# Chunked attention and a top-2 mixture of experts: the rest list summed by routing group in the last attention slot, turned tiles amid the first products, and nine result rows' puts behind the overflow branch

## The chip, the cores and the metric

The kernel runs on one core of a Trainium2 chip. The metric is the device time of one execution in microseconds (us). Engines are named as the profile does: PE (matmul; PEld its weight loads), DVE, ACT, POOL and SP; a q behind a name is that engine's sequencer. POOL issues all gathers and scatters (indirect DMAs), SP the transposing DMAs and the direct stores.

## The reference

First an attention over chunks of 32 queries, each of which sees 8 memory keys and the keys from 16 before its chunk to 8 behind it; then a mixture of experts over the 3072 tokens that come out.

```
q, k, v: 4 batches x 8 heads x 768 x 64;  mem_k, mem_v: 8 keys each
for each chunk c: a = softmax(q_c . [mem_k, k_ctx] / 8);  out_c = a . [mem_v, v_ctx]
x = out as (3072, 512)
noisy = x @ w_gate + log1p(exp(x @ w_noise)) * noise          # 8 experts
top2 of noisy per token, their weights by softmax over the two
for e in 8 experts, for the tokens that chose e:
    out[token] += weight * (relu(x[token] @ w1[e]) @ w2[e])   # 512 -> 1024 -> 512
```

## The kernel before, in words

**Phase 1** runs 12 attention tiles in slots. In each slot a string of short codes (`ORDERS`) says in which order the pieces of work are written, and each engine runs its instructions in that order. Tokens are routed in three groups of tiles: tiles 0 to 6, 7 to 9, and 10 to 11 (the last group, whose tiles carry names such as `d_last`, `vals_last`). The last slot's string holds the routing of groups 1 and 2.

**Sorting.** The tokens are listed by the pair of experts that they chose (28 pairs). The first 96 tokens of a pair make one ordinary tile; `main_src` holds the token numbers of each tile's rows, as sums of one-hot matrices times facts (`p_list`). Tokens beyond the 96 of their pair are the rest. They are listed in the same way: `rest_onehots` (L1204 to L1207) makes one-hots of 64 rest positions for all 24 subtiles of 128 tokens at once, `rest_list` (L1214) multiplies them with the facts in 24 matmuls, the sum is copied to `tsb` and stored to `tdr` in DRAM, and 16 small gathers (`rest_facts`) bring each expert's rest entries to `fr`. `rest_decode` makes of them the row numbers from which to read (`rs`), those to which to write (`rd`, in pieces `dA` and `dB`) and the weights; `rest_rows` gathers the rows. If any count is too large for its place, `flag` is above zero, and a branch behind everything else runs `overflow()`, which repairs the result.

**Phase 2** goes through the experts. `gathers` brings token tiles from `xd` in DRAM into `xt` (POOL, L938, one indirect DMA per tile), a tile is turned, that is transposed, either by an SP transposing DMA or by PE with a copy (`turn_pe`, L1148 and L1149), `mm1` (L992) makes the hidden rows (relu at L978 on DVE, L980 on ACT), `mm2_tiles` (L1054) the results. A pair's tile is made once by each of its two experts; the second one adds (L1063) and its rows are put to the output (`put`, L943, POOL). Rest rows are added to what the output holds: `clear_prev` clears `pA` and `pB` (ACT, L1124), `get_prev` reads the rows (POOL, L969), `ins_` adds them (`yB` L1108, `yr` L1117) and `put_rest` (L960) writes them back. Four tiles of opposite pairs (names `yq`, `QP`) are finished by `finish_q` (L1085, L1086). `later` is the list of finished rows whose puts `flush` issues.

The head of phase 2 is written out by hand (L1385 on): seven gathers, the counts and tables of the rest (`rest_counts`, `rest_tables`), the rest one-hots, tile 0 turned and multiplied, tiles 1 and 2 turned, the rest list, a product over tiles 1 and 2 (192 columns), tile `QP` turned, the 32-column products, the three tiles of `i0` turned, and then the product over these three (288 columns). For the last expert (e = 7) the rest rows are put first and then the three results of `in_of(7)`, before the branch; behind the branch, which stands in `tc.If(nov > 0)` and is taken or not by all engines, stand the three results of `out_of(7)` and the last `yq`.

A wait in this kernel is a count that an engine's instruction waits for; an instruction that waits holds all that is behind it on its engine. PE, ACT, DVE, SP and POOL all run in the written order here.

Of the kernel before, what the change touches and what calls it, by code (L numbers as in the profile page):

```python
# [22 lines left out]
def kernel(  # L23
# [73 lines left out]
    NV = 6  # L97
# [85 lines left out]
    radr = const.tile([128, 2, E], F32, name="radr")  # L183
    rslot28 = const.tile([128, 2], F32, name="rslot28")
# [80 lines left out]
    class Route:  # L265
# [397 lines left out]
    def decode(L, n, name, src=None, pool=const):  # L663
# [42 lines left out]
    ]  # L706

    with tc.manual_schedule(engines={ET.PE, ET.Activation, ET.DVE, ET.SP}):
# [32 lines left out]
        def slot(i):  # L741
# [133 lines left out]
            for k in ORDERS[i + 1].split():  # L875
# [4 lines left out]
                elif k == "p2":  # L880
                    p2 = new_list(NV - 2)
                elif k == "a":
# [14 lines left out]
            if i == NT - 1:  # L897
                add_list(p1, 0, 1)
                add_list(p2, 1, NV - 1)

# [83 lines left out]
    def mm1(e, cols, x, sinks, engs=(0, 1)):  # L984
        fk = 1 if cols > 256 else 2 if cols > 128 else 4
        for f0 in range(0, FB, fk):
            p = psH.tile([128, 512], F32, name="p_h")
            for f in range(f0, f0 + fk):
                o = p[:, (f - f0) * cols:(f - f0 + 1) * cols]
                for kp in range(KP):  # L990
# [3 lines left out]
                                     start=(kp == 0), stop=(kp == KP - 1))  # L994
            for c0, c1, to in sinks:
# [54 lines left out]
    def mm2_tiles(e, ps, h, unit):  # L1050
        for k, g in enumerate(ps):
# [9 lines left out]
            else:  # L1061
# [3 lines left out]
                later.append((y[0:MT], dst[0:MT, g:g + 1]))  # L1065

    def flush():
        for y, ix in later:
            put(y, ix)
        later.clear()  # L1070

    def outs(e):
        unit = yqp.tile([128, Dm], F32, name="yq") if e < 4 else yrp.tile([128, Dm], F32, name="yr")
        mm2_tiles(e, out_of(e), hO, unit)
        if e < 4:
            yq[e] = unit
        else:
            yr_of[e] = unit

    def finish_q(e):  # L1080
        if e >= 4:
# [3 lines left out]
            nc.vector.tensor_scalar(out=y, in0=y, scalar1=wl[0:MT, 0, q:q + 1], scalar2=None, op0=Alu.mult)  # L1085
            last[0] = nc.vector.scalar_tensor_tensor(out=y, in0=unit[0:MT], scalar=wl[0:MT, 1, q:q + 1], in1=y, op0=Alu.mult, op1=Alu.add)  # L1086
            later.append((y, dst[0:MT, q:q + 1]))
# [6 lines left out]
    def ins_(e):  # L1094
# [18 lines left out]
        put_rest(rest_tile(), dB, outB, 2 * N)  # L1113
# [4 lines left out]
        put_rest(unit[0:MT], dA, out, N)  # L1118
# [25 lines left out]
    def turn_pe(g, to, n=MT):  # L1144
# [4 lines left out]
        nc.scalar.copy(to, p)  # L1149
# [8 lines left out]
    tsb = late.tile([RU, NP, 8], F32, name="tsb")  # L1158
    oh_at = scol[0] + 4096
    oh_t = wflat[:, oh_at:oh_at + NG * RU].rearrange("p (g t) -> p g t", g=NG)  # L1160
# [10 lines left out]
    def rest_tables(p, part):  # L1171
# [28 lines left out]
        nc.vector.tensor_copy(nxt, flag)  # L1200

    def rest_onehots():
        t1 = late.tile([128, NG], F32, name="t1")
        nc.vector.tensor_scalar(out=t1, in0=rank, scalar1=float(MT), scalar2=None, op0=Alu.is_ge)  # L1204
        k2 = late.tile([128, NG], F32, name="k2")
# [317 lines left out]
```

## Time and profile before

| what | us |
|---|---|
| median of 3 runs (lowest to highest) | 346.47 (346.16 to 347.88) |
| the profiled execution's own time | 349.4 |
| its span, first to last instruction | 347.8 |
| PE busy (80% of the span) | 278.9 |
| POOL busy (58%) | 203.4 |
| DVE busy (53%) | 183.6 |
| ACT busy (45%) | 155.0 |

The profiled execution took 2.9 us longer than the median, and 1.6 us of its own time lie outside its span. Phase 1 lasts to about 130 us, the head of phase 2 to about 150; from there PE works nearly without a pause until 329, and the span ends at 347.8 with nothing but POOL's puts behind it. The mean granted clock of TensorE is 0.918. Shares of busy time are averages over these stages, so a change is to be read from the stage that it touches. In the profile's rows the first number is the start in us, the second the duration in us; brackets hold how long the engine was idle before and what released it.

### The profile page before, as it was taken

The page shows a single profiled execution, that of the slowest core. Times are in us where ns is not written, and L with a number is a line of the kernel's source. Part 1 is how long each engine was busy: PE and PEld are TensorE (multiplying, and loading weights), DVE is VectorE, ACT ScalarE, POOL GpSimd, SP SyncE. Part 2 cuts the span into 40 slices and gives each one's busy share as a digit, 9 for nine tenths or more (in the row PEclk, how much of TensorE's full clock was granted, in tenths as well). Part 3 has the DMA queues.
Part 4 walks back from the last instruction along what each step waited for, and adds up shares of the span by engine and source line. Part 5 has one row for each costly group of instructions (what it writes and reads, how often), then busy time and mean ns, then how long its engine had stood idle before and what let it go on. Part 6 is the DMA issues. An engine that isn't in the chain of part 4 may idle for free.

```text
span 347.8 us, 9190 instructions
## 1 busy us (share of the span) xinstructions
PE 278.9 (80%) x3746; PEld 207.2 (60%) x3762; DVE 183.6 (53%) x406; ACT 155.0 (45%) x320; POOL 203.4 (58%) x291
## 2 busy tenths in 40 slices
PE   0678788766777746797999999999999999999800
PEld 0557677655667636656668766676676666866300
DVE  4675568676499677236363533644345354353500
ACT  4657638553565312534445363553443534534200
POOL 4669679982046247745777776571745735626531
PEclk9978899998899556999999999999999999999955
DMA  7999969999516512421686996999999699504221
GB/s 127 211 211 179 224 111 210 192 168 161 106 28 107 140 31 59 109 59 47 114 119 139 160 127 158 185 217 166 186 150 198 159 170 157 152 25 118 79 77 45
DMA packets 43277, 46.78 MB, mean 135 GB/s; under 512 B 20241, under 2 KB 33621, under 8 KB 43228
## 3 DMA queue, kind: packets, MB, share of 16 engines
q0 software_dynamic: 22800, 38.26, 58.8%
q1 hardware_dynamic: 19884, 7.83, 11.6%
q8 instruction: 31, 0.51, 0.6%
q14 instruction: 18, 0.15, 0.1%
q10 hardware_dynamic: 544, 0.03, 0.1%
HBM read 59.11 MB, written 11.33 MB: 203 GB/s over the span
## 4 chain that ended last, share of the span: by engine, by line
PE 44%; issue 6%; DMA 5%; DVE 4%; POOL 2%; ACT 2%; POOLq 1%; DVEq 0%; ACTq 0%
PE p_h L992 23%; PE p_y L1054 17%; DMA pB<-out_dram,ri 4%; POOL out_dram L943 2%; PE p_y L1102 2%; ACT w_all L1149 1%; DMA xt<-xd,main_src 1%; ACT w_all L980 1%; PE p_xt L1214 1%; DVE yq L1048 0%; POOLq L1518 0%; PE p_x L623 0%; POOL out_dram L960 0%; PE p_xt L1148 0%; PE p_list L372 0%
## 5 line engine op out<-in xcount | busy, mean ns | idle before, releaser
L992 PE MATMUL p_h<-w_all 128*128 128x288 bf16 (+3 forms) x1120 | 96.1, 248 | 4.0 <-ACT w_all L1149 2.8
L992 PEld LDWEIGHTS <-w_all 128*128 128x128 bf16 x1120 | 83.1, 99 | 17.7 <-issue 5.9
L1054 PE MATMUL p_y<-w_all 128*128 128x512 bf16 x368 | 83.6, 379 | 1.7 <-ACT yr L1048 0.5
L980 ACT ACTIVATE w_all<-p_h 128x288 bf16<-128x288 f32 (+3 forms) x137 | 46.8, 375 | 51.8 <-PE p_h L992 50.3
L1054 PEld LDWEIGHTS <-w_all 128*128 128x128 bf16 x384 | 37.0, 98 | 43.3 <-issue 1.8
L412 POOL COPY w_all<-w_all 128x512 bf16<-128x512 bf16 (+1 forms) x59 | 42.0, 781 | 13.0 <-PE p_t L432 8.4
L978 DVE TENSOR_SCALAR w_all<-p_h 128x288 bf16<-128x288 f32 (+1 forms) x65 | 30.7, 476 | 35.5 <-PE p_h L992 34.0
L938 POOL DMA_INDIRECT xt<-xd,main_src x28 | 27.0, 963 | 10.1 <-issue 7.3
L1063 DVE SCALAR_TENSOR_TENSOR y<-p_y,main_w,y 96x512 f32<-96x512 f32 x24 | 17.9, 747 | 24.8 <-PE p_y L1054 24.8
L943 POOL DMA_INDIRECT out_dram<-y,main_dst x24 | 22.5, 936 | 12.6 <-issue 6.1
L1048 ACT COPY yr<-p_y 32x512 f32<-32x512 f32 x24 | 13.9, 579 | 35.6 <-DVE y L1063 34.5
L960 POOL DMA_INDIRECT out_dram<-yB,rd x8 | 9.8, 1226 | 28.6 <-DVE yB L1108 28.0
L1059 ACT ACTIVATE y<-p_y,main_w 96x512 f32<-96x512 f32 x24 | 16.4, 682 | 21.2 <-PE p_y L1054 20.1
L432 PE MATMUL p_t<-identf,w_all 128*128 128x128 f32 x120 | 20.6, 314 | 1.3 <-ACT pT L587 0.8
L938 POOL DMA_INDIRECT xt<-xd,rs x16 | 14.8, 924 | 11.3 <-DVE rw L1246 6.3
L1048 DVE COPY yr<-p_y 32x512 f32<-32x512 f32 x12 | 8.3, 694 | 22.3 <-ACT y L1059 21.3
L614 DVE TENSOR_TENSOR w_all<-ps_o,rs 128x512 bf16<-128x512 f32 x24 | 15.7, 683 | 6.5 <-PE ps_o L601 5.6
L1223 POOL DMA_INDIRECT fr<-tdr,adr x16 | 16.1, 1007 | 4.9 <-issue 4.9
L461 PE MATMUL p_v<-identf,w_all 128*128 128x128 f32 x96 | 15.9, 305 | 2.7 <-ACT w_all L436 1.8
L432 PEld LDWEIGHTS p_t<-identf,w_all 128*128 128x128 f32 x120 | 15.9, 163 | 2.7 <-POOL w_all L412 1.4
L587 ACT COPY pT<-p_p 128x1024 bf16<-128x1024 bf16 x11 | 11.1, 1012 | 12.7 <-PE p_p L581 12.4
L501 DVE TENSOR_REDUCE mx<-ps_s 128x16 f32<-128x1024 f32 x12 | 14.7, 1223 | 2.8 <-PE ps_s L488 2.5
(231 smaller groups left out, 405.2 us busy)
## 6 DMA issues: line engine op xcount, KB each, us to landing
w_all<-in_moe_w_dram POOLq DMA_DIRECT2D x16, 1024.0 KB
w_all<-in_k_dram POOLq DMA_DIRECT2D x4, 768.0 KB
w_all<-in_q_dram POOLq DMA_DIRECT2D x4, 768.0 KB
w_all<-in_v_dram POOLq DMA_DIRECT2D x4, 768.0 KB
xd<-w_all SPq DMA_DIRECT2D x24, 128.0 KB
w_all<-mvn SPq DMA_DIRECT2D x24, 32.0 KB
w_all<-xt SPq DMA_TRANSPOSE x39
xt<-xd,main_src POOLq DMA_INDIRECT x28
```

Source lines behind the costliest of these rows:

```text
L412: i = eng.tensor_copy(to, x)
L432: nc.tensor.transpose(out=p_t[:, s, :], in_=m.bitcast(F32)[:, s * 128:(s + 1) * 128], identity=identf)
L938: pin(nc.gpsimd.indirect_dma_start(out=t[0:n].bitcast(I32), out_offset=None, in_=src_, in_offset=bass.IndirectOffsetOnAxis(ap=ix, axis=0)))
L943: i = nc.gpsimd.indirect_dma_start(out=out if rows is None else rows, out_offset=bass.IndirectOffsetOnAxis(ap=ix, axis=0), in_=y, in_offse ...
L978: nc.vector.tensor_scalar(out=out_, in0=in_, scalar1=0.0, scalar2=None, op0=Alu.max)
L980: nc.scalar.activation(out=out_, in_=in_, func=Act.Relu)
L992: nc.tensor.matmul(out=o if len(xk.shape) == 2 else o.rearrange("p (j t) -> p j t", j=xk.shape[1]), lhsT=w_all[:, e % WR, kp * F + f * 128 ...
L1048: (nc.scalar.copy if eng else nc.vector.tensor_copy)(to, p[MT:128, :])
L1054: nc.tensor.matmul(out=p, lhsT=h[:, f, k, :], rhs=w2(e, f), start=(f == 0), stop=(f == FB - 1))
L1059: nc.scalar.activation(out=y[0:MT], in_=p[0:MT], func=Act.Copy, scale=wt)
L1063: nc.vector.scalar_tensor_tensor(out=y[0:MT], in0=p[0:MT], scalar=wt, in1=y[0:MT], op0=Alu.mult, op1=Alu.add)
L1223: i = nc.gpsimd.indirect_dma_start(out=fr[0:n, b, e], out_offset=None, in_=tdr, in_offset=bass.IndirectOffsetOnAxis(ap=adr[0:n, b, e:e + 1 ...
```

## The change

- The rest list is made by routing group. `rest_onehots(r)` and `rest_list(r, p)` take one group; codes `I0`, `I1`, `I2` (one-hots of group 0, 1, 2) and `T0`, `T1`, `T2` (their matmuls) stand in the last slot's string, the sum stays in a PSUM tile of phase 1 and is copied to `tsb` at the slot's end. The store of `tsb` is SP's first work of phase 2.
- In the head, tile 0 is turned first. Tiles 1, 2, `QP` and `i0` are turned amid the matmuls of the product before them (`amid`), some of the copies go to DVE.
- `away` is −128 where `flag` is zero, and far out of the output's rows where it is not, so that rest rows are not put when the branch will be taken.
- For e = 7 the puts of the three `in_of(7)` results, of `yB` and of `yr` move behind the branch, where there are nine instead of four. For e = 6 the three results are put ahead of the rest rows. `scale_q` (L1085 of before) stands ahead of `outs(e)`.
- The first part of the rest's decode stands amid `outs(0)`, the rest rows' gathers follow it ahead of one tile of `in_of(1)`, and the rest rows of expert 0 are turned amid `mm1_rest(1)`.

```diff
-        "P N p X C1 C1 V i x v G X2 ... H2 O2 q2 a B2 F2",
+        "P N p X C1 C1 V i I0 x v G X2 ... H2 O2 I1 q2 T0 T1 a B2 F2 I2 T2",
...
+    def rest_onehots(r):
+        t1 = keep.tile([128, r.n], F32, name=f"t1{r.k}")
+        nc.vector.tensor_scalar(out=t1, in0=r.rr, scalar1=float(MT), scalar2=None, op0=Alu.is_ge)
+        k2 = keep.tile([128, r.n], F32, name=f"k2{r.k}")
+        nc.vector.scalar_tensor_tensor(out=k2, in0=r.rr, scalar=1.0 - MT, in1=t1, op0=Alu.add, op1=Alu.mult)
+        nc.vector.tensor_tensor(out=oh_t[:, r.g0:r.g0 + r.n], in0=bc(k2, RU),
+                                in1=io_1[:, 0:RU].unsqueeze(1).to_broadcast([128, r.n, RU]), op=Alu.is_equal)
+    def rest_list(r, p):
+        for s in range(r.n):
+            g = r.g0 + s
+            nc.tensor.matmul(out=p, lhsT=oh_t[:, g], rhs=r.vals[:, s], start=(g == 0), stop=(g == NG - 1))
...
             if i == NT - 1:
                 add_list(p1, 0, 1)
                 add_list(p2, 1, NV - 1)
+                nc.vector.tensor_copy(tsb[:, :, 0:NV], p_rest.rearrange("p v c -> p c v"))
...
-    def mm1(e, cols, x, sinks, engs=(0, 1)):
+    def mm1(e, cols, x, sinks, engs=(0, 1), amid={}):
...
+                if f in amid:
+                    amid[f]()
...
-        put_rest(rest_tile(), dB, outB, 2 * N)
+        if e == E - 2:
+            flush()
+        yB = rest_tile()
+        later_rest = [partial(put_rest, yB, dB, outB, 2 * N), partial(put_rest, unit[0:MT], dA, out, N)]
+        if e < E - 1:
+            later_rest.pop(0)()
...
-        put_rest(unit[0:MT], dA, out, N)
+        if e < E - 1:
+            later_rest.pop(0)()
+        later.extend(later_rest)
...
+        nc.vector.tensor_scalar(out=away, in0=flag, scalar1=float(BIG), scalar2=-128.0, op0=Alu.mult, op1=Alu.add)
...
-        nc.vector.scalar_tensor_tensor(out=t, in0=t, scalar=-128.0, in1=u, op0=Alu.add, op1=Alu.max)
+        nc.vector.scalar_tensor_tensor(out=t, in0=t, scalar=away, in1=u, op0=Alu.add, op1=Alu.max)
...
+        rest_store()
+        turn_pe(0, xs[:, 0])
         p_cnt = rest_counts()
         rest_tables(p_cnt, 0)
-        rest_onehots()
-        turn_pe(0, xs[:, 0])
-        mm1_main(0, [0], hO, engs=(0,))
-        turn_pe(1, xs[:, 1])
-        turn_pe(2, xs[:, 2])
-        p_t = rest_list()
-        mm1(0, 2 * MT, ..., engs=(0,))
-        turn_pe(QP, x3[0][:, :, 0:MT])
-        mm1_rest(0, r=False, engs=(0,))
-        nc.vector.memset(tsb, 0.0)
+        mm1_main(0, [0], hO, engs=(0,), amid={3: lambda: turn_pe(1, xs[:, 1], eng=0), 5: lambda: turn_pe(2, xs[:, 2])})
         rest_tables(p_cnt, 1)
-        rest_store(p_t)
...
+        mm1(0, 2 * MT, ..., engs=(0,),
+            amid={1: lambda: turn_pe(QP, x3[0][:, :, 0:MT]), 4: lambda: turn_pe(i0[0], xs[:, i0[0]], eng=0),
+                  6: lambda: turn_pe(i0[1], xs[:, i0[1]], eng=0)})
         next(dec)
+        mm1_rest(0, r=False, engs=(0,), amid={3: lambda: turn_pe(i0[2], xs[:, i0[2]], eng=0)})
         dst, wl = next(dec)
-        for g in i0:
-            turn_pe(g, xs[:, g])
...
-        i1 = gathers(in_of(1))
-        outs(0)
+        i1 = gathers(in_of(1), 2)
         dx = rest_decode(0, 2)
-        next(dx)
-        next(dx)
+        outs(0, amid={1: lambda: next(dx)})
         rest_rows(0)
+        i1 += gathers(in_of(1))
         rest_rows(1)
+        next(dx)
...
             if n == E:
                 ins_(e)
-                flush()
+            scale_q(e)
             outs(e)
```

**DVE at the end of the last slot.** Here `d_last`, `facts` and `vals_last` are the last group's facts, `listed` the sums of the lists. Before:

```order
L336 TENSOR_TENSOR d_last<-d_last,facts 128x4
L334 CAST facts<-d_last 128x4
L337 TENSOR_TENSOR facts<-ii_last 128x4
L366 TENSOR_TENSOR vals_last<-ohp,facts 128x4x112
L384 TENSOR_TENSOR listed<-listed,p_list 96x28
L384 TENSOR_TENSOR listed<-listed,p_list 96x112
L1174 TENSOR_SCALAR cnt_2956<-p_xt 128x64
```

After:

```order
L341 TENSOR_TENSOR d_last<-d_last,facts 128x4
L339 CAST facts<-d_last 128x4
L342 TENSOR_TENSOR facts<-ii_last 128x4
L371 TENSOR_TENSOR vals_last<-ohp,facts 128x4x112
L387 TENSOR_SCALAR t_2946<-rank 128x4
L389 SCALAR_TENSOR_TENSOR k_2948<-rank,t_2946 128x4
L390 TENSOR_TENSOR w_all<-k_2948,io_128 128x256
L402 TENSOR_TENSOR listed<-listed,p_list 96x28
L402 TENSOR_TENSOR listed<-listed,p_list 96x112
L925 COPY tsb<-ps_o 64x28x6
L1214 TENSOR_SCALAR cnt_2999<-p_xt 128x64
```

The one-hots of the last group's rest (L387 to L390) and the copy to `tsb` stand ahead of the counts. In the built program the first gather of phase 2 (POOL) waited for DVE's count behind `main_src`; now it waits for the count behind L390, since its tile `xt` lies where `k_2948` lay.

**ACT at the head of phase 2.** The L1149 rows of before and the L454 rows of after with `p_xt` are copies of turned tiles. Before:

```order
L1149 COPY w_all<-p_xt 128x384
L980 ACTIVATE w_all<-p_h 128x4x96 x2
L1149 COPY w_all<-p_xt 128x384 x2
L980 ACTIVATE w_all<-p_h 128x2x2x96 x4
L1149 COPY w_all<-p_xt 128x4x96
L980 ACTIVATE w_all<-p_h 128x12x32 x2
L679 ACTIVATE main_w<-main_w 128x56
L1149 COPY w_all<-p_xt 128x384 x3
L980 ACTIVATE w_all<-p_h 128x3x96 x4
```

After:

```order
L454 COPY w_all<-p_xt 128x384
L1006 ACTIVATE w_all<-p_h 128x4x96
L454 COPY w_all<-p_xt 128x384
L1006 ACTIVATE w_all<-p_h 128x4x96
L454 COPY w_all<-p_xt 128x4x96
L1006 ACTIVATE w_all<-p_h 128x2x2x96 x4
L697 ACTIVATE main_w<-main_w 128x56
L1006 ACTIVATE w_all<-p_h 128x12x32 x2
L1006 ACTIVATE w_all<-p_h 128x3x96 x4
```

Tile 2 is copied between the two relus of tile 0's product, `QP` ahead of the first relu of the 192 columns, and the four copies of tile 1 and `i0` are gone to DVE.

**POOL at the tail.** `pA` and `pB` are the reads of the rows that the rest is added to, `nxt` is the flag as a number. Before:

```order
L969 DMA pA<-out_dram,ri_4379 96x512
L969 DMA pB<-out_dram,ri_4379 128x256
L960 DMA out_dram<-yB,rd_4377 6144x256
L960 DMA out_dram<-yr,rd_4377 3072x512
L943 DMA out_dram<-y,main_dst 3072x512 x3
L1488 TENSOR_LOAD nxt
L1490 COMPARE_AND_BRANCH
...
L943 DMA out_dram<-y,main_dst 3072x512 x3
L943 DMA out_dram<-yq,main_dst 3072x512
```

After:

```order
L995 DMA pA<-out_dram,ri_4391 96x512
L995 DMA pB<-out_dram,ri_4391 128x256
L1506 TENSOR_LOAD nxt
L1508 COMPARE_AND_BRANCH
...
L969 DMA out_dram<-y,main_dst 3072x512 x3
L986 DMA out_dram<-yB,rd_4389 6144x256
L986 DMA out_dram<-yr,rd_4389 3072x512
L969 DMA out_dram<-y,main_dst 3072x512 x3
L969 DMA out_dram<-yq,main_dst 3072x512
```

Five puts moved from ahead of the branch to behind it, and the branch now follows the read of `pB`.

More of the change, by code (lines that the diff above doesn't have):

```diff
@@ L1 @@
 import math
+from functools import partial
 from contextlib import ExitStack
@@ L1157 @@
     nxt = late.tile([128, 1], I32, name="nxt")
-    tsb = late.tile([RU, NP, 8], F32, name="tsb")
-    oh_at = scol[0] + 4096
-    oh_t = wflat[:, oh_at:oh_at + NG * RU].rearrange("p (g t) -> p g t", g=NG)
+    away = late.tile([128, 1], F32, name="away")
     def rest_counts():
@@ L1435 @@
         load_next()
-        for b, n, c in ((0, MT, MT), (1, RU, 2 * MT)):
-            turn_pe(("r", 0, b), x3[0][:, :, c:c + n], n)
         turn_rest(1)
```

62 lines of the change are left out of this document (33 added, 29 removed), and 2 rows, old and new, of the table ORDERS.

## The prediction

> **What bounds the kernel now.** I read the table of stretches first (us, then busy time of PE, PEld, DVE, ACT, POOL, the granted clock, DMA share and GB/s), then the chain of waits through the head of phase 2, then the rows around the branch.
>
> ```profile
> 118.50:123.50 5.00, 2.72 (x29) 2.35 (x30) 4.25 (x14) 1.39 (x5) 4.04 (x10) 0.50 0.19 43
> ...
> 130.40:137.30 6.90, 4.56 (x62) 4.18 (x62) 5.42 (x22) 1.20 (x3) 5.60 (x5) 0.50 0.20 58
> 137.30:147.10 9.80, 7.28 (x110) 6.79 (x108) 3.66 (x20) 5.69 (x14) 7.40 (x8) 1.00 0.44 107
> ...
> 182.50:300.00 117.50, 116.75 (x1020) 79.62 (x1028) 53.15 (x107) 53.07 (x133) 71.52 (x74) 1.00 0.93 168
> ...
> 330.00:347.80 17.80, 0.00 (x0) 0.00 (x0) 1.12 (x2) 0.58 (x1) 4.16 (x5) 0.55 0.22 65
> ```
>
> From 182.5 to 300 PE is the bound (116.75 of 117.5 us), and the change touches nothing there: what is won or lost ahead of 182.5 goes through to the end unshortened. It can act in three places. In the last slot DVE is the bound (4.25 of 5.00 us). In the head PE works 11.8 of 16.7 us and waits for tiles and copies. From 330 on PE is idle, and 17.8 us belong to POOL. The head, by the chain of waits (its small steps of issue between these lines are left out):
>
> ```profile
> 130.44 2.71 DMA xt<-xd,main_src
> 133.20 0.52 PE p_xt L1148 x4
> 133.79 0.49 ACT w_all L1149
> 134.31 2.73 PE p_h L992 x32
> 137.46 0.48 ACT w_all L1149
> 137.98 1.90 PE p_xt L1214 x24
> 139.88 2.76 PE p_h L992 x32
> 143.15 0.38 ACT w_all L1149
> 143.57 1.53 PE p_h L992 x32
> 146.18 0.34 PE p_xt L1148 x4
> 147.08 4.08 PE p_h L992 x32
> ```
>
> Tile 0 is gathered, turned, copied, multiplied; then PE stands while ACT copies the next tile, and so on. From the landing of tile 0 (130.44 + 2.71 = 133.15) to the first product of `in_of(0)` at 147.08 it is 13.93 us. The tail, POOL's rows and the last result of DVE by the timeline, then the sequencer's instructions of the branch (L1490) and of the end (L1518), with count, shortest, median and longest in ns and first and last start:
>
> ```profile
> 319.75 1.03 POOL L969 DMA_INDIRECT pB<-out_dram,ri  x1 [0.30 <-issue]
> 324.21 1.27 POOL L960 DMA_INDIRECT out_dram<-yB,rd  x1 [3.42 <-DVE yB L1108]
> 325.78 0.95 POOL L960 DMA_INDIRECT out_dram<-yr,rd  x1 [0.30 <-issue]
> 329.49 1.00 POOL L943 DMA_INDIRECT out_dram<-y,main_dst  x1 [0.30 <-issue]
> 335.41 0.92 POOL L943 DMA_INDIRECT out_dram<-y,main_dst  x1 [4.92 <-DVEq L1490]
> 339.08 0.92 POOL L943 DMA_INDIRECT out_dram<-yq,main_dst  x1 [0.30 <-issue]
> 330.63 0.75 DVE L1086 SCALAR_TENSOR_TENSOR yq<-yr,main_w,yq 96x512 f32<-96x512 f32 x1 [0.25 <-ACT yr L1048]
> ```
>
> ```profile
> L1490 POOLq EVENT_SEMAPHORE  x6: 17/30/43, 329.9 to 332.6; - x6
> L1490 POOLq COMPARE_BRANCH  x1: 58/58/58, 327.2 to 327.2; - x1
> L1490 POOLq INC_SWDGE_SEM  x1: 1795/1795/1795, 332.7 to 332.7; - x1
> L1518 POOLq DRAIN  x3: 46/109/9904, 337.0 to 347.5; - x3
> ```
>
> The branch costs POOL 4.92 us in which it does nothing. It compares at 327.2, its next instruction stands at 329.9 (2.6 us later), then six semaphore waits go to 332.6, which is 3.2 us after the last put ahead of the branch began (329.49), then INC_SWDGE_SEM takes 1.80 us to 334.5, and 0.9 us later the first put behind the branch starts. I read the waits as those for the landing of everything that POOL issued before. The last result is ready at 330.63 + 0.75 = 331.38, so the end is set by POOL's branch and its four puts. The long DRAIN begins at 337.0 (337.0 + 9.9 is 346.9, and a later start would not fit into the span), 6.9 us past the last put's end at 340.0.
>
> **The change, part by part.**
>
> *Tail: the branch is taken earlier.* Ahead of the branch now stands the read of `pB` (319.75) as the last transfer. The nearest rows for its landing are 2.71 us (the first gather) and 3.2 us (the last put): 322.5 to 323.0. POOL's compare can follow that read's issue at about 320, plus 2.6 us to the next instruction gives 322.7, much the same. So INC starts at about 322.8, ends at 324.6, and the first put starts at 325.5. Nine puts follow. Each `y` starts 1.22 us after the one before (0.92 + 0.30), `yB` takes 1.57 (1.27 + 0.30) and `yr` 1.25: three `y` 3.66, `yB` and `yr` 2.82, three `y` 3.66, together 10.1 us to the start of the last, 335.6 instead of 339.08. That is −3.4. The results are there in time: `yB` before 324.21 (its put began then), `yq` at 331.4. Bounds: −3.9, if the pieces lie closer, to −2.5, if the wait behind the branch costs a further us.
>
> *Smaller pieces of the tail.* `scale_q` leaves DVE's end; nothing follows, since `yq` waits for its turn on POOL. For e = 6 the three `y` are put ahead of the rest rows, and `pA` waits for `yr` to land; POOL has 3.42 us idle ahead of `yB` before, and the read of `pA` waits for the same `clear_prev` on ACT either way. Zero; if that cover were gone, the read of `pB`, and so the branch, would come later by about one put, 1.22 us.
>
> *Last slot: one-hots added on DVE.* These rows price them:
>
> ```profile
> 127.91 0.56 DVE L359 TENSOR_TENSOR oh_l_last<-rank,io_l 128x384 bf16<-128x384 f32 x1
> 129.37 0.18 DVE L883 TENSOR_TENSOR main_src<-p_list,listed 96x28 int32<-96x28 f32 x1 [0.91 <-PE p_list L372]
> 130.56 0.16 DVE L337 TENSOR_TENSOR facts<-ii_last 128x4 bf16<-128x4 f32 x1
> 130.76 0.63 DVE L366 TENSOR_TENSOR vals_last<-ohp,facts 128x448 bf16<-128x448 bf16 x1
> 133.04 0.21 DVE L1204 TENSOR_SCALAR t<-rank 128x24 f32<-128x24 f32 x1
> 133.29 0.18 DVE L1206 SCALAR_TENSOR_TENSOR k<-rank,t 128x24 f32<-128x24 f32 x1
> 133.50 1.76 DVE L1207 TENSOR_TENSOR w_all<-k,io 128x1536 bf16<-128x1536 f32 x1
> ...
> 130.44 1.05 POOL L938 DMA_INDIRECT xt<-xd,main_src  x1 [1.89 <-DVE d_last L336]
> ```
>
> 384 columns take 0.56 and 1536 take 1.76, about 1.04 ns per column. `I0` (896 columns) is 0.21 + 0.18 + 1.09 = 1.48, written into the stretch where DVE has 0.75 of 5.00 us idle: +1.4 (bounds +0.7 and +1.5). `I1` (384 columns) is 0.95 and falls into the 0.91 us idle ahead of `main_src`: +0.1. `I2` (256 columns, 0.43 + 0.39 = 0.82) stands behind `vals_last`, and by the order of the built program the first gather waits for it, since its tile lies on the memory of the one-hots' input. Before, the gather started at 130.44, 0.89 us after `main_src` (129.55); the count that it waits for is that of `main_src`, though the row names a later DVE instruction. Now DVE comes through `facts` and `vals_last` to 131.4 and through `I2` to about 132.1 (the pieces overlap by 0.1), and with the same 0.89 the gather starts at 133.0 instead of 130.44: +2.6 (bounds +1.7 without the 0.89, +2.7). Together the first gather moves by +4.1. The matmuls of `T0` to `T2` (24 of 79 ns, from 1.90 us) lie beside DVE's work.
>
> *Head: turned tiles amid the products.* From the landing of tile 0 in the new order: turning 0.52, copy 0.49, gaps 0.09, then 2.73 for tile 0's product with two turnings amid it (0.52 each at the half clock, 0.34 at the full: 0.9 together), then 2.76 for the 192 columns with three turnings (1.0), then 1.53 + 0.34 for the 32 columns with one, and about 0.3 of gaps: 10.6 instead of 13.93. Gone are the 1.90 of the rest list and three copies on which PE stood (0.48, 0.38 and 0.49 with the gaps around them). −3.3; bounds −2.3 (one copy or one landing still waited for in each product) and −3.9. The gathers of `i0` follow each other like the puts, about 1.22 us apart, and fall due about when they are turned. The rest's tables stand behind tile 1's copy on DVE; the `i0` copies stand behind those tables, about 20 small instructions of 0.2, and PE's next tile hides them as long as the 192 columns last. Together slot and head: +0.8 (bounds −1.0 and +2.0).
>
> *Clock of the head.* In the table PE's granted clock is 0.50 up to 137.3 and 1.00 from there, 4.1 us after the turning of tile 0 began at 133.20. I take the same 4.1 us at half clock from the new start. The Trainium skill (TensorE: Matmul & The Clock Gate, Part 1) says that the gate opens only after a busy window of about 3.4 us, and that the windows run freely, so that the place of the change depends on where work begins in a window. By that rule the cold stretch lies between 3.4 and 6.8 us, the row's 4.1 fits it, and the sum would be up to 1.2 us longer in an execution that starts unluckily; only the change of clock at 137.3, in one execution, is shown here.
>
> *Rest decode and rest rows.*
>
> ```profile
> 158.95 0.21 ACT L1249 ACTIVATE rx<-rx 128x8 f32<-128x8 f32 x1 [1.82 <-DVE rx L1248]
> ...
> 159.51 0.77 PE L992 MATMUL p_h<-w_all 128*128 128x288 bf16 x5 [1.14 <-ACT w_all L980]
> ...
> 164.27 0.92 PE L992 MATMUL p_h<-w_all 128*128 128x160 bf16 x11 [0.89 <-ACT w_all L1149]
> ```
>
> PE waits 1.14 us at 159.51 for a relu that ACT reaches only after an exponential of the decode (L1249, itself 1.82 us late), and 0.89 at 164.27 for copies of the rest rows. With the decode's first part amid `outs(0)` and the turnings amid the products a part of both goes: −0.35 each, −0.7 in all (bounds 0, if POOL's gathers or the transposes behind them are late next, and −1.5). The extra `away` is one DVE instruction of about 0.2 on a flag that nobody waits for before the tail: hidden. The store of `tsb`, first on SP's queue now, waits for DVE's copy; SP has no transposes due until later in the head.
>
> *Sum.* Tail −3.4, slot and head +0.8, rest −0.7: −3.3 us. The profiled execution took 349.4, its span 347.8; the changed one comes to a span of 344.5. The profiled one lies 2.9 above the median of 346.47, so I take the difference to the median: 346.47 − 3.3 = 343.2.
>
> **Rivals.**
>
> 1. *The first put behind the branch is released by DVE's branch, not by POOL's own.* Its row names DVEq L1490, and that instruction and POOL's INC end together at 334.5, so times alone can't tell them apart. Then nothing is won by an earlier compare: DVE's branch can't come before its last result, the first put stays at 335.4, and five more puts (3 × 1.22 + 1.57 + 1.25 = 6.5) follow: 349.7 with the other terms, slower. Against it: in the built program that put waits for DVE's count of the `y`, which stands below that of `yq`, and for a DMA count that INC raises. The same sign would come from a DRAIN that grows with the number of puts behind the branch: its 6.9 us by four puts are 1.7 each, five more are +8.7, and above 0.7 each the gain is lost. Nothing varies that number in the trace.
> 2. *The later gather isn't bought back.* If PE still waits for landings or copies in the head, its gain is the bound −2.3 (1.0 worse); if the decode's waits only move to POOL's gathers, 0.7 is lost as well; both give 344.9, no change that can be told, and with a half clock that lasts a window's part longer still more. For it speaks that the head's gathers come one by one from POOL, 4.1 us later than before; against it, that PE's waits there are for copies in the quoted rows of the chain and for a landing only in the first.
> 3. *The tail gains less.* If something else holds the branch (the landing of `pA`, or a branch target that takes longer than 2.6 us), by 1.5 us: 344.7.
> 4. *The front gains as well.* If `I0` falls into DVE's idle time (+0.7) and decode and head reach their good bounds, 343.2 − 0.7 − 0.6 − 0.8 = 341.1.
>
> **How the numbers follow.** 0.5% is 1.73 us, about what a measurement of this kernel can tell from no change: below 344.74 is faster, above 348.2 slower. My forecast, 342.0 to 344.5, has 0.56; rival 4 has 0.10, all faster; rival 3 has 0.12, two thirds of it faster; rival 2 has 0.14, a quarter of it faster; rival 1 has 0.08, all slower. Faster 0.56 + 0.10 + 0.08 + 0.03 = 0.77, slower 0.08, no change 0.15. The range reaches from rival 4 with a little more on its side, 340.5, to the upper part of rival 2, 345.8; what it leaves out is rival 1 and tails of 2 and 4, under 0.2.
>
> **What would show it.** In the profile after: the first put behind the branch near 325.5 plus the shift of the front, nine puts to about 335.6, and the end 6.9 us past the last; the first gather near 134.5; the stretch from its landing to the 288-column product near 10.6 us; no L1214 of before between products. The prediction is wrong if the first put behind the branch waits for the end of DVE's work, if the DRAIN is longer than 9 us past the last put, or if PE shows waits for copies by DVE in the head.

## The result

The changed kernel took 343.62 us (median of 20 runs, 341.86 to 347.81), the kernel before beside it 348.67 (20 runs, 346.16 to 351.90). The ratio is 0.9871, 95% interval 0.9843 to 0.9898: 1.0 to 1.6% faster. On the median of 346.47 that the forecast started from, the ratio gives 342.0; forecast were 343.2, with a range of 340.5 to 345.8. The profiled execution's span went from 347.8 to 343.7 us.

The tail of the changed kernel, POOL's timeline from the reads of `pA` and `pB` on, then the sequencer's instructions at the branch (now L1508) and at the end (L1536):

```profile
317.31 1.00 POOL L995 DMA_INDIRECT pA<-out_dram,ri  x1 [3.93 <-ACT pA L1166]
318.61 1.04 POOL L995 DMA_INDIRECT pB<-out_dram,ri  x1 [0.30 <-DVE y L1091]
324.55 0.96 POOL L969 DMA_INDIRECT out_dram<-y,main_dst  x1 [4.91 <-DVE yq L1114]
...
329.58 1.45 POOL L986 DMA_INDIRECT out_dram<-yr,rd  x1 [0.30 <-issue]
...
335.01 0.92 POOL L969 DMA_INDIRECT out_dram<-yq,main_dst  x1 [0.31 <-issue]
```

```profile
L1508 POOLq EVENT_SEMAPHORE  x6: 17/30/43, 321.4 to 321.9; - x6
...
L1508 POOLq COMPARE_BRANCH  x1: 58/58/58, 318.3 to 318.3; - x1
...
L1508 POOLq INC_SWDGE_SEM  x1: 1695/1695/1695, 321.9 to 321.9; - x1
...
L1508 DVEq EVENT_SEMAPHORE  x1: 21/21/21, 333.3 to 333.3; - x1
...
L1536 POOLq DRAIN  x3: 46/109/12603, 330.3 to 343.4; - x3
```

POOL compares at 318.3, its INC runs from 321.9 to 323.6, and the first of nine puts starts at 324.55. The read of `pB` began at 318.61, and the six semaphore instructions at the branch take 0.5 us (321.4 to 321.9), where before they took 2.7 us (329.9 to 332.6), with puts issued just ahead of them: in the changed kernel next to nothing is left to wait for there. DVE's instruction of the branch, which the row of before named as the releaser, stands at 333.3, 8.7 us after the first put. The last put ends at 335.93 and the span 7.8 us later, as before (339.99 and 347.8).

The head, by the chain of waits (small steps of issue left out):

```profile
133.41 2.75 DMA xt<-xd,main_src
136.20 0.50 PE p_xt L1190 x4
...
137.31 1.44 PE p_h L1018 x16
138.75 0.32 PE p_xt L1190 x4
139.07 0.64 PE p_h L1018 x8
139.71 0.32 PE p_xt L1190 x4
140.03 2.00 PE p_h L1018 x16
...
145.89 4.70 PE p_h L1018 x48
```

The last row joins two things: the second half of the 32-column products (16 matmuls) and the product over `in_of(0)` (32 matmuls of 288 columns). In PE's timeline the latter begins at 146.50:

```profile
146.50 0.42 PE L1018 MATMUL p_h<-w_all 128*128 128x288 bf16 x2
```

The copies by ACT that stood between the products of before are gone from the chain; in these rows a turning costs PE its own 0.32 (0.17 at the full clock) and nothing more.

Phase 1 takes a different time in each execution: the reciprocal with which DVE begins the part of the last slot that is compared here stood between 114.6 and 119.9 us in the fourteen profiles, the kernel before at 118.46. Whole spans of single executions are therefore compared by stretches between six landmarks of the timeline: that reciprocal (R), the start of the first gather of phase 2 (G), the first result product (Y), the end of the last matmul (Z), the end of the last put (T), the end of the span (E).

| us | R to G | G to Y | Y to Z | Z to T | T to E | sum |
|---|---|---|---|---|---|---|
| before | 11.98 | 20.77 | 177.99 | 10.80 | 7.80 | 229.34 |
| changed | 15.71 | 17.02 | 177.62 | 7.88 | 7.77 | 226.00 |
| difference | +3.73 | −3.75 | −0.37 | −2.92 | −0.03 | −3.34 |

In these two executions the front takes and gives the same, and what is won is the tail. In the second, third and fourth sets of runs every kernel, the one before too (medians 432.65, 432.25 and 433.84 us), took some 80 us longer than in the first; of these only stretches that are free of it are read.

### The profile page after: what moved, and what is told of

The parts are those of the page before. It is cut to its first block, busy times and chain, and to the rows that moved or that the text cites. A ratio compares the mean times of both kernels' runs of the same rounds, so it can differ in the third digit from the quotient of the medians.

```text
span 343.7 us, 9215 instructions
## 1 busy us (share of the span) xinstructions
PE 285.3 (83%) x3762; PEld 212.9 (62%) x3762; DVE 185.8 (54%) x417; ACT 153.6 (45%) x316; POOL 203.2 (59%) x291
## 4 chain that ended last, share of the span: by engine, by line
PE 47%; DMA 11%; DVE 9%; issue 6%; POOL 3%; ACT 2%; POOLq 1%; DVEq 0%; ACTq 0%
PE p_h L1018 21%; PE p_y L1082 15%; DMA w_all<-in_moe_w_dram 3%; DMA fr<-tdr,adr 2%; DMA out_dram<-yr,rd 2%; DMA w_all<-mvn 2%; PE p_t L450 2%; PE p_y L1137 1%; DMA pB<-out_dram,ri 1%; POOL out_dram L969 1%; PE ps_o L396 1%; DVE w_all L632 1%; POOL out_dram L986 1%; PE ps_s L506 1%; PE p_x L641 1%
## 5 line engine op out<-in xcount | busy, mean ns | idle before, releaser
L1018 PE MATMUL p_h<-w_all 128*128 128x288 bf16 (+3 forms) x1120 | 98.0, 249 | 1.5 <-ACT w_all L1006 0.9
L1082 PE MATMUL p_y<-w_all 128*128 128x512 bf16 x384 | 85.9, 379 | 1.0 <-DVE yq L1076 0.6
L964 POOL DMA_INDIRECT xt<-xd,main_src x28 | 26.2, 936 | 12.8 <-issue 7.6
L479 PE MATMUL p_v<-identf,w_all 128*128 128x128 f32 x96 | 16.6, 315 | 2.5 <-ACT w_all L454 1.8
L454 ACT COPY w_all<-p_v 128x512 f32<-128x512 f32 x21 | 11.9, 588 | 8.1 <-PE p_v L479 8.1
```

What stands on the lines that cost most here:

```text
L479: nc.tensor.transpose(out=p_v[:, i, c, :], in_=vT[:, c, c0:c0 + 128], identity=identf)
L964: pin(nc.gpsimd.indirect_dma_start(out=t[0:n].bitcast(I32), out_offset=None, in_=src_, in_offset=bass.IndirectOffsetOnAxis(ap=ix, axis=0)))
L1018: nc.tensor.matmul(out=o if len(xk.shape) == 2 else o.rearrange("p (j t) -> p j t", j=xk.shape[1]), lhsT=w_all[:, e % WR, kp * F + f * 128 ...
L1082: nc.tensor.matmul(out=p, lhsT=h[:, f, k, :], rhs=w2(e, f), start=(f == 0), stop=(f == FB - 1))
```

## The experiments

Kernels of the first set ran beside runs of the kernel before with a median of 349.39 us.

**tail_only**: the kernel before with the tail's part alone.

```diff
-        put_rest(rest_tile(), dB, outB, 2 * N)
+        if e == E - 2:
+            flush()
+        yB = rest_tile()
+        later_rest = [...]          # as in the changed kernel; e = 7 puts them behind the branch
...
                 ins_(e)
-                flush()
+            scale_q(e)
```

> The kernel before with the tail's part alone: nine puts behind the branch, the rest rows masked, the e = 6 puts ahead of the rest rows, scale_q early. My theory: the branch waits for the landing of what POOL issued before, so with the read of pB as the last transfer the first put behind it starts near 325.5, the last ends near 336.5 and the span about 6.9 us behind that: -3.0 to -3.4 us, a ratio of 0.990 to 0.991. Rival (DVE's branch releases the puts): first put past 334, nine puts to 345, ratio 1.02. Rival (the time of the change was won in the front): ratio 0.997 or more.

Ratio 0.9933 (0.9893 to 0.9972). Its tail by POOL's timeline, and the closing DRAIN:

```profile
318.52 1.04 POOL L970 DMA_INDIRECT pB<-out_dram,ri  x1 [0.30 <-DVE y L1064]
324.44 0.96 POOL L944 DMA_INDIRECT out_dram<-y,main_dst  x1 [4.89 <-DVE yq L1085]
...
329.49 0.93 POOL L961 DMA_INDIRECT out_dram<-yr,rd  x1 [0.30 <-issue]
...
334.40 0.92 POOL L944 DMA_INDIRECT out_dram<-yq,main_dst  x1 [0.30 <-issue]
```

Z to T is 7.36 us, 3.44 less than before, and T to E 7.78. The first put comes 5.92 us after the read of `pB` began, as in the changed kernel (5.94). The half us between 7.36 and the changed kernel's 7.88 is one put: `yr` took 0.93 here and 1.45 there. The rival of DVE's branch falls (it had the first put past 334). The other, a gain of the front, had 0.997 or more and stands at the edge of the interval; by the stretches the tail's gain is there.

Ahead of the tail this profile shows how far single executions differ. G to Y is 21.39 us and Y to Z 178.48, 0.62 and 0.49 longer than before, and the head's code is that of before. PE began to turn tile 0 at 130.84, and the half clock lasted until 137.41, 6.6 us, where it lasted 4.1 in the profile before; the 24 matmuls of the list took 2.75 us instead of 1.90. The stretch ahead of the change of clock:

```profile
134.00:137.41 3.41, 3.10 (x31) 3.01 (x29) 2.51 (x15) 1.24 (x3) 2.77 (x3) 0.50 0.32 91
```

So differences of half a microsecond between single profiles say nothing in these two stretches.

**head_only**: the changed kernel with the old tail (the diff of tail_only, undone).

> The changed kernel with the old tail: rest list in the last slot, turned tiles amid the products, rest decode amid outs(0). My theory: the first gather comes 3.7 us later and the stretch from its landing to the first product over in_of(0) is 9.7 instead of 13.9 us, with -0.7 for the rest: -0.5 to -1.3 us, ratio 0.996 to 0.9985. Rival (front and tail each give half): ratio 0.993. Rival (the front costs, as forecast before): ratio 1.000 to 1.002.

Ratio 0.9958 (0.9918 to 0.9997). By stretches: R to G 15.71, G to Y 17.06, Y to Z 177.68, Z to T 10.89, sum 229.14, −0.20 to before. The stretches up to Z are those of the changed kernel to within 0.06 us and show no gain in the front; the timed runs show some, between nothing and 0.8%, which leaves the rival of 0.993 open. The two parts multiply to 0.9933 × 0.9958 = 0.9891, inside the changed kernel's interval.

**no_amid**: the list stays in the last slot, the turned tiles stand as before, with their copies back on ACT.

```diff
-        mm1_main(0, [0], hO, engs=(0,), amid={3: ..., 5: ...})
+        mm1_main(0, [0], hO, engs=(0,))
+        turn_pe(1, xs[:, 1])
+        turn_pe(2, xs[:, 2])
...
+        turn_pe(QP, x3[0][:, :, 0:MT])
+        mm1_rest(0, r=False, engs=(0,))
...
+        for g in i0:
+            turn_pe(g, xs[:, g])
```

> The changed kernel with the head's turned tiles in the order before (tiles 1 and 2 between the products, QP and i0 behind them, copies on ACT); the list stays in the last slot. My theory: the late first gather stays (+3.7), but of the 4.2 us won behind it only the 1.9 of the rest list's matmuls and some of its waits are left: about +2 us against the changed kernel, ratio to before 0.993. Rival (the turning amid products only moves PE's waits): no difference to the changed kernel, 0.987.

Ratio 0.997 (0.9932 to 1.0009): worse than the 0.993 expected, and the rival of 0.987 falls. G to Y is 21.33, 4.31 more than in the changed kernel and 0.56 more than before, though the list's matmuls are gone from it. PE's timeline shows why: it waits for each copy again, and the product over 192 columns, 2.76 us before, takes 4.85.

```profile
138.82 4.85 PE L1018 MATMUL p_h<-w_all 128*128 128x192 bf16 x32 [0.69 <-ACT w_all L454]
143.51 0.34 PE L1190 MATMUL p_xt<-identb,xt 96*128 96x96 bf16 x4
144.62 1.52 PE L1018 MATMUL p_h<-w_all 128*128 128x96 bf16 x32 [0.78 <-ACT w_all L454]
```

The clock tells the rest. These are stretches of 3.41 us laid on the places where the granted clock changed (PE busy is the first number behind the length, the clock the third from the end). Before:

```profile
130.44:133.85 3.41, 1.57 (x23) 1.20 (x23) 2.11 (x10) 0.06 (x1) 2.80 (x3) 0.50 0.20 58
133.85:137.26 3.41, 2.94 (x38) 2.94 (x38) 3.24 (x13) 1.10 (x3) 2.80 (x3) 0.50 0.21 58
137.26:140.67 3.41, 2.97 (x41) 2.80 (x39) 2.30 (x15) 1.05 (x3) 2.50 (x4) 1.00 0.32 81
```

The changed kernel:

```profile
129.31:132.72 3.41, 3.41 (x27) 3.14 (x26) 2.94 (x14) 0.00 (x0) 0.00 (x0) 0.50 0.00 0
132.72:136.14 3.42, 0.69 (x8) 0.42 (x7) 0.59 (x2) 0.00 (x0) 2.12 (x3) 1.00 0.17 46
136.14:139.55 3.41, 3.12 (x48) 3.06 (x49) 0.67 (x3) 0.97 (x2) 2.64 (x3) 0.50 0.32 92
139.55:142.97 3.42, 3.42 (x32) 3.24 (x31) 3.07 (x20) 1.55 (x4) 2.67 (x3) 0.50 0.31 85
142.97:146.38 3.41, 3.41 (x65) 3.41 (x62) 2.12 (x12) 1.93 (x6) 2.50 (x4) 1.00 0.28 70
```

no_amid:

```profile
132.85:136.26 3.41, 2.37 (x39) 2.31 (x40) 1.50 (x10) 0.49 (x2) 2.50 (x4) 0.50 0.30 85
136.26:139.68 3.42, 2.73 (x30) 2.53 (x28) 3.07 (x20) 1.72 (x4) 2.50 (x4) 0.50 0.28 80
139.68:143.09 3.41, 3.41 (x23) 3.13 (x22) 0.05 (x1) 1.21 (x3) 2.58 (x3) 0.50 0.30 87
```

In the changed kernel the matmuls of the list and of `p_list` fill a stretch (3.41 of 3.41 us), and in the next one, in which PE waits for the first gather (0.69 of 3.42), the clock is full; then it is half again for 6.83 us. In no_amid PE stands for copies (2.37 and 2.73 us busy), and the half clock lasts three stretches, 10.24 us. So of the 4.31 us a part is waits for copies, and a part is the 3.41 us that the half clock lasts longer. Whether the waits for copies keep the clock half for longer, or chance in this execution does, isn't shown.

**both**: two edits to the changed kernel.

```diff
-        t1 = keep.tile([128, r.n], F32, name=f"t1{r.k}")
+        t1 = const.tile([128, r.n], F32, name=f"t1{r.k}")
-        k2 = keep.tile([128, r.n], F32, name=f"k2{r.k}")
+        k2 = const.tile([128, r.n], F32, name=f"k2{r.k}")
-        "S M W P X y s W p y L x l V i v E G v1 r",
+        "S M W P X y s W p y L x l V i I0 v E G v1 r",
-        "P N p X C1 C1 V i I0 x v G ...
+        "P N p X C1 C1 V i x v G ...
```

> The changed kernel with two edits: the one-hots' inputs t1 and k2 lie in memory that no later tile takes, so that the first gather waits for main_src alone, and I0 stands in the slot before, where DVE idles 1.94 us. My theory: the first gather starts near 129.5 to 130.5 instead of 133.4, and all of it comes through, -2.5 and -1.2: 3.7 us below the changed kernel, ratio to before 0.976. Rival (the gather isn't what holds PE, since the matmuls of T2, the counts and the half clock stand there): 1 us or less, 0.984 or more.

Ratio 0.9732 (0.9678 to 0.9787), well below the changed kernel. R to G is 11.86 us, that of the kernel before, G to Y 15.97, Z to T 7.35, and the sum 220.68, 8.66 below before. DVE's timeline in the slot before, and POOL's first gather:

```profile
109.90 0.25 DVE L627 RECIPROCAL rs<-ps_g 128x16 f32<-128x16 f32 x1
...
110.49 1.09 DVE L390 TENSOR_TENSOR w_all<-k,io 128x896 bf16<-128x896 f32 x1
112.36 0.69 DVE L632 TENSOR_TENSOR w_all<-ps_o,rs 128x512 bf16<-128x512 f32 x1 [0.78 <-PE ps_o L619]
```

```profile
127.78 1.05 POOL L964 DMA_INDIRECT xt<-xd,main_src  x1 [1.88 <-DVE facts L339]
```

`I0` fits into the wait for `ps_o`, of which 0.78 us are left. The gather lands while the list's last matmuls still run, and PE goes straight on. By the table of stretches the clock that is full after them stays so:

```profile
127.93:131.34 3.41, 3.41 (x33) 2.82 (x31) 2.13 (x9) 0.00 (x0) 2.80 (x3) 0.50 0.20 53
131.34:134.75 3.41, 2.88 (x60) 2.56 (x58) 1.87 (x11) 1.84 (x4) 2.50 (x4) 1.00 0.35 94
```

G to Y is 1.05 us shorter than in the changed kernel, which I had not expected and which fits this clock.

The next kernels are those of the sets that took longer: PE, DVE and ACT stand still in phase 2, for up to some 10 us at a time, with nothing in the profile that they wait for. POOL goes on issuing gathers meanwhile. ACT's timeline of early_I0 shows one such place:

```profile
142.27 0.49 ACT L1006 ACTIVATE w_all<-p_h 128x384 bf16<-128x384 f32 x1 [8.90 <-remote]
```

In these profiles G to Y is 30.3 to 33.6 us for all kernels, so nothing is read from it or from their ratios. All the ratios that these kernels gave lie above what was expected; whether the stops alone make that isn't shown. The stretches that have no such stop agree with the first set: R to G is 15.72 and 15.70 us where the slot is that of the changed kernel (three_less, no_branch), Z to T 7.31 to 7.88 where the tail is, T to E 7.5 to 7.8. From such stretches alone the following is read.

**free_gather** and **early_I0**: each of the two edits of both alone.

> The changed kernel with the inputs of the rest's one-hots (t1, k2) in memory that no later tile takes; I0 stays in the last slot. My theory: the first gather waits for main_src alone and starts 2.6 us earlier after the last slot's reciprocal (13.1 instead of 15.71 us), and it all comes through: 2.5 us below the changed kernel, ratio to before 0.980. Rival (the earlier gather finds PE with the list's matmuls, and PE's first turning waits for them): 1 us or less, 0.984.

> The changed kernel with I0 written into the slot before, behind the reciprocal there, where DVE idles 1.94 us; the one-hots' inputs stay. My theory: the stretch from the last slot's reciprocal to the first gather shrinks from 15.71 to 14.4 us, the slot before stays as long: 1.3 us below the changed kernel, ratio to before 0.983 to 0.984. Rival (I0 in the slot before delays that slot's norm by as much): no difference, 0.987.

Ratios 0.9893 (0.9847 to 0.9939) and 0.9992 (0.9937 to 1.0046). R to G is 13.06 us with the gather freed, 2.65 less than 15.71, as expected; it is 14.92 with `I0` moved, 0.79 less where 1.3 were expected.

**no_list** and **no_list_2**: the list back in the head, turned tiles amid the products.

```diff
...                                 # t1 and k2 in const as in both; I0 to I2 and T0 to T2 out of the slot's string
-        rest_store()
-        turn_pe(0, xs[:, 0])
         p_cnt = rest_counts()
         rest_tables(p_cnt, 0)
+        for r in R:
+            rest_onehots(r)
+        turn_pe(0, xs[:, 0])
         mm1_main(0, [0], hO, ...)
+        p_rest = psX.tile([128, NV, NP], F32, name="p_xt")[0:RU]
+        for r in R:
+            rest_list(r, p_rest)
...
```

> The changed kernel with the rest list back in the head (one-hots on DVE behind the counts, the 24 matmuls behind tile 0's product), turned tiles amid the products as in the changed kernel. My theory: the first gather comes 3.7 us earlier again, the list costs 1.9 us on PE in the head and holds DVE's copy of tile 1 for its 2.2 us of one-hots: about 1 us below the changed kernel, ratio to before 0.984. Rival (moving the list is what won the head): 2 us above the changed kernel or more, 0.993.

> The same kernel as in the run no_list (rest list back in the head, turned tiles amid the products), again, for the same reason. My theory: from the last slot's reciprocal to the first gather 11.9 us instead of 15.7, from there to the first result product 1.9 to 2.9 us more than the changed kernel's 17.0: 1 to 2 us below the changed kernel, ratio to before 0.982 to 0.985. Rival (the move of the list is what won the head): the stretch to the first result product is longer by more than the 3.8 us, ratio 0.987 or more.

Ratio 0.9899 (0.9867 to 0.9932) in the first; the second (six runs of 417.23 to 427.59 us) gave none. R to G is 11.85 and 12.02 us, so the 3.7 us come with the list in the last slot. What the list costs in the head drowned in the stops. Whether the move of the list pays by itself stays open.

**best** and **best_2**: both's two edits, and the clear of `pA` and `pB` earlier for e = 7.

```diff
+            if n == E:
+                clear_prev(e)
             mm1_main(e, in_of(e), hI)
-            clear_prev(e)
+            if n < E:
+                clear_prev(e)
```

> The changed kernel with both edits (gather free of the one-hots, I0 in the slot before) and, for e = 7, pA and pB cleared ahead of the product over in_of(7) instead of behind it. My theory: ACT's clear is what the read of pA waits for (3.93 us idle on POOL), so pA is read 1.7 us earlier, once yr of e = 6 has landed, and with it come the branch and all nine puts: 1.2 to 1.7 us below the kernel with the two edits (0.9732), ratio to before 0.969. Rival (the puts wait for their results then): 0.5 us or less, 0.972; if ACT's clear delays PE by as much as it wins, 0.973.

> The same kernel as in the run best (one-hots' inputs apart, I0 in the slot before, pA and pB cleared ahead of the product over in_of(7)), again, since in that run every kernel stood still in phase 2 for some 80 us. My theory as there: 1.2 to 1.7 us below the kernel with the two edits, ratio to before 0.969; the read of pA starts 3.2 us behind the start of the put of yr of e = 6, where it stood 4.9 us behind it. Rival: the clear delays PE by what it wins, 0.973.

Ratios 0.9879 (0.9807 to 0.9952) and 0.9785 (0.9712 to 0.9857). POOL's timeline of best_2:

```profile
389.45 0.92 POOL L986 DMA_INDIRECT out_dram<-yr,rd  x1 [0.30 <-issue]
393.05 0.99 POOL L995 DMA_INDIRECT pA<-out_dram,ri  x1 [2.69 <-ACT w_all L1006]
```

The read of `pA` starts 3.60 us after the put of `yr` instead of 4.9 in the first set and 6.1 to 6.2 in the other kernels of these. So the clear was what held the read, and with it the branch. Z to T is 4.86 in both runs instead of 7.3 to 7.9, but that is too much: in these sets PE's stops fall between the put of `yr` and Z and make the latter 1.3 us later (16.9 us from one to the other, 15.6 in both). Counted from the put of `yr` to the end of the last put it is 21.96 and 21.91 us, against 22.96 in both (305.83 to 328.79). My estimate from this is that the clear is worth 1.0 us in undisturbed runs, a little less than the 1.2 to 1.7 expected; it wasn't timed.

**three_less**: three puts fewer behind the branch.

```diff
+        del later[0:3]
         flush()
```

> The changed kernel without the puts of the three in_of(7) results (six puts behind the branch; 288 rows of the output miss a term). My theory: POOL issues the puts behind the branch one every 1.22 us and these set the end: the last put ends 3.7 us earlier unless it waits for yq, and the end stays 7.8 us behind it: 3.0 to 3.7 us below the changed kernel, ratio to before 0.977. Rival (the closing DRAIN grows with the puts): the end is then nearer than 7.8 us to the last put, by 1 us or more. Rival (results set the end): 1 us or less, 0.984.

The 288 rows are put once each, so here they are not written at all, where the expectation has them miss a term. Ratio 0.9884 (0.983 to 0.9938). Z to T is 4.20 us, 3.68 less than the 7.88 of the kernels that, like this one, have a single put of 1.3 to 1.5 us. That is three puts of 1.22: the rate of the puts sets the end. Its DRAIN begins and ends so:

```profile
L1537 POOLq DRAIN  x3: 46/109/8672, 414.9 to 424.2; - x3
```

414.9 + 8.7 is 423.6, 6.7 us after the last put's end at 416.88. After four puts it was 6.9 (before, 339.99 to 346.9), after nine 6.9 (changed, 335.93 to 342.9): it doesn't grow with them.

**no_branch**: the branch and the repair left out.

```diff
-        with tc.If(nov > 0):
-            overflow()
         flush()
```

> The changed kernel without the branch and the repair behind it (a list that overflows would not be repaired), the nine puts straight behind the read of pB. My theory: what the branch still costs is the 4.9 us in which POOL stands between pB and the first put, less what the puts then wait for their results: the last put goes out right behind yq, 4 to 4.7 us earlier, ratio to before 0.974. Rival (nothing is left to win, the rate of the puts sets the end): 1 us or less, 0.984.

Ratio 0.9937 (0.9887 to 0.9986). The first put starts 1.34 us after the read of `pB` began (403.70 to 405.04), where it is 5.9 to 6.1 with the branch: some 4.6 us earlier. In this profile the end doesn't follow by as much. The last put ends 14.87 us after the start of that read, 1.9 to 2.5 less than in the kernels with nine puts behind a branch (16.75 to 17.33), since later puts wait for results, 1.94 us ahead of one `y`. But DVE made that `y` late, after 2.10 us in which it waited for nothing that the profile shows:

```profile
413.76 1.41 DVE L1091 SCALAR_TENSOR_TENSOR y<-p_y,main_w,y 96x512 f32<-96x512 f32 x2 [2.10 <-remote]
414.78 0.92 POOL L969 DMA_INDIRECT out_dram<-y,main_dst  x1 [1.94 <-DVE y L1091]
```

So how much of the 4.6 us would reach the end in an undisturbed run stays open. Z to T, 4.32 us, doesn't tell it, since Z itself comes 18.0 us behind the start of the put of `yr` of e = 6 here and 16.9 in other kernels of these sets.

## Why the prediction was right, point by point

*Tail, −3.4.* Measured −2.92 in the changed kernel's profile and −3.44 with the tail alone. The reading of the branch held in the main: POOL's own INC releases the puts, and what it issued before had landed by 321.9, 3.3 us after the read of `pB` began (2.7 to 3.2 were the bounds); INC took 1.70 instead of 1.80. The step from the compare was not as forecast: the compare ran at 318.3, ahead of that read and not at 320 behind it, and 3.1 us passed to the next instruction (321.4) instead of 2.6. What sets these 3.1 us isn't shown. The nine puts took 10.46 us from first to last start where 10.1 were forecast, since `yr` took 1.45 (the row of before: 0.95).

*Last slot, +4.1.* Measured +3.73. Its terms: `I0` takes its 1.12 us and DVE's norm follows the reciprocal 1.56 us later instead of 0.34 (118.46 to 118.80 before), +1.22 where +1.4 stood, of which 1.07 are left at the last one-hots (L364 starts 10.52 us after the reciprocal, before 9.45); `I1` costs nothing (from those one-hots to `main_src` it is 1.47 us, before 1.46); and the gather's wait for `I2` is +2.65 (3.72 us from `main_src` to the gather, 1.07 before) against +2.6. free_gather's −2.65 confirms the last term, and with it the reading of the built program against the profile, which names another releaser in both kernels (in the changed one a matmul of the list).

```profile
117.70 0.25 DVE L627 RECIPROCAL rs<-ps_g 128x16 f32<-128x16 f32 x1
...
118.22 1.12 DVE L390 TENSOR_TENSOR w_all<-k,io 128x896 bf16<-128x896 f32 x1
119.26 0.68 DVE L632 TENSOR_TENSOR w_all<-ps_o,rs 128x512 bf16<-128x512 f32 x1
...
128.22 0.56 DVE L364 TENSOR_TENSOR oh_l_last<-rank,io_l 128x384 bf16<-128x384 f32 x1
...
129.69 0.18 DVE L908 TENSOR_TENSOR main_src<-p_list,listed 96x28 int32<-96x28 f32 x1
...
133.41 1.05 POOL L964 DMA_INDIRECT xt<-xd,main_src  x1 [4.53 <-PE ps_o L396]
```

*Head, −3.3.* From the landing of tile 0 (136.16) to the product over `in_of(0)` (146.50) it is 10.34 us, forecast 10.6, before 13.93: −3.59, within the bounds. (The 9.7 in the expectation of head_only was read from the joined row at 145.89.) From the first gather to the first result product the gain is 3.75. It came in spite of the half clock, which was forecast at 4.1 us and lasted 6.83, so some term beside the clock was better than forecast. By the Trainium skill (TensorE: Matmul & The Clock Gate, Part 1) a busy window of about 3.4 us opens the clock, and where in a window the work begins decides when. The trace agrees on the length of 3.41 us, and tail_only, with the head of before, shows 6.6 us at half clock for 4.1 and a G to Y that is 0.62 longer, inside the 1.2 that I allowed for. But a window with 3.12 of 3.41 us busy did not open it in the changed kernel, while one with 2.94 did before, and in no_amid it stayed shut for three windows, longer than the 6.8 us that I worked out from the page.

*Rest decode and rest rows, −0.7.* Y to Z is 0.37 shorter; PE's wait of 1.14 us became 0.86 and that of 0.89 became 0.46, together 0.71 as forecast. Whether the other half was given back later can't be told, since before and tail_only differ by 0.49 in this stretch.

```profile
158.66 2.80 PE L1018 MATMUL p_h<-w_all 128*128 128x288 bf16 x32 [0.86 <-ACT w_all L1006]
...
162.99 2.37 PE L1018 MATMUL p_h<-w_all 128*128 128x160 bf16 x32 [0.46 <-DVE rg L1287]
```

*Rivals.* The first (DVE's branch releases the puts, or the DRAIN grows) is refuted by the changed kernel's rows and by three_less. Its time was added up wrong: 349.7 is 346.47 + 6.5 with the whole −3.3, which has the tail's −3.4 in it; with the other terms alone (+0.8 and −0.7) it is 353.1. Either is slower, so the chances stand. The second and third did not come: the head's gain was above its lower bound, and in the tail the sum was off by 0.5 us, most of it the one slow put of `yr`. Slot and head together were forecast at +0.8 and measured at −0.02 in one execution; head_only's timed ratio puts them and the rest at −0.1 to −2.9 us.

*The sum.* Forecast −3.3, by stretches −3.34. That these agree to the tenth is luck: the three terms were off by +0.5 (tail), −0.8 (slot and head) and +0.3 (rest), which cancel. The timed ratio says −4.5 (−3.6 to −5.5 on a base of 349). The difference of about 1 us lies ahead of R or is the luck of single profiles, such as the clock: its half stretch was short (4.1 us) in the profile before, and 6.6 and 6.8 us long in those of tail_only and the changed kernel. The runs do not tell which, since R itself moved by 5 us between executions.

## What to carry to other kernels

A tile pool's reuse of memory is a wait that no line of the code shows: two small tiles in a pool that is freed held the first gather of the next phase for 2.65 us, and giving them memory of their own, with the one-hots of `I0` moved into a measured idle stretch, was worth about as much again as the whole change (0.9732 against 0.9871). Where an engine must pass a branch, look at what it issued last before: by the rows of before the branch waited for the puts ahead of it to land, so put long-waiting stores behind it and let the reads ahead of it start early. And in the changed kernel work that filled PE just before it had to wait bought a full clock that was gone when the data came.

## What the runs showed of the hardware

The branch costs POOL 4.85 to 5.07 us from the end of its last issue to the next put in all thirteen profiles that have it (4.92 before, 4.91 changed), of which 1.7 to 1.8 are INC_SWDGE_SEM; without it the gap is 0.30 us (no_branch). The closing DRAIN lasts 6.7 to 6.9 us beyond the last put whether four, six or nine stand behind the branch. In the changed kernel the granted clock changes at 132.72, 136.14 and 142.97 us, one and two times 3.41 us apart, and the stretch after 3.41 us of busy PE had the full clock though PE worked 0.69 us in it. How busy a stretch must be isn't shown: after one of 2.94 us the clock was full (before), after one of 3.12 it was half. And the same program took 346 us in one set of runs and 430 in others, with stops of up to some 10 us on PE, DVE and ACT; why is open.
